# Two small edits at the ends of a tensor-bound kernel: a separate bank for the last half block, and narrower constant matmuls in the setup

## The chip, the cores and the metric

One NeuronCore of a Trainium2 chip. The metric is the device time of one execution in microseconds (us). The span in a profile is about 1.7 us shorter than the time of the same run (217.3 against 219.02 us before, 218.6 against 220.28 after). TensorE, VectorE, ScalarE and GpSimd are PE, DVE, ACT and POOL in the profile; SP is the engine that issues most transfers (111 of 120 in the profile of before).

## The reference, cut to what matters

A block-wise linear attention (4 batches, 8 heads, 768 tokens, head size 64) feeds a feed-forward layer with weights of 512 x 2048 and 2048 x 512.

```python
intra = einsum('bhic,bhjc->bhij', qb, kb) * Dmask     # scores inside a block
out   = einsum('bhij,bhjd->bhid', intra, vb) + (qb * lam_pow) @ kv_state
kv_state = lam_block * kv_state + kb_dec^T @ vb
x = out as (3072 tokens, 512)
h = x @ w_in;  g = h * cos(h);  y = g @ w_out
```

## The kernel before: the parts that matter

The kernel works on 24 blocks of 128 tokens. A planner in Python puts tasks of all engines in one order. The parts that the change and the argument touch:

```python
DMA_FROM = 8                      # from this block on q and k are transposed by DMA
...
def transposes_dma():             # block n >= DMA_FROM
    nc.sync.dma_start_transpose(out=new_T()..., in_=live["qk", n]...)
...
def scores():                     # waits for the transposed q and k of block n
    t = bank("ps_s", [P, 2, NP, P], F32)
    ... 8 matmuls of 128 columns ...
...
# last block: two column halves, both in the two-bank tile ps_s
live["f", i, j] = [bank("ps_s", [P, 2, DM], F32)[:, x, :width] for x in range(2)]
...
def keep_awake(us, at):           # constant matmuls while the setup has no work for the tensor engine
    for _ in range(int(us / (4 * P / (1200.0 if at < 5.0 else 2400.0) + 0.0025))):
        nc.tensor.matmul(idle_ps, lhsT=ident, rhs=blank, start=True, stop=True)
```

`keep_awake` is meant to keep the array's clock up until the first layer begins. It writes zeros that nobody reads.

## Time and profile before

| | before |
|---|---|
| time, four runs on the chip of the record, in order of size | 218.53, 218.69, 218.74, 222.54 us |
| span of the profiled run (a fifth run, of 219.02 us) | 217.3 us |
| tensor engine busy | 206.5 us, 95% |
| first matmul of the first layer | 21.21 us |
| wait for the DMA transpose of block 10 | 68.7 to 70.65 us |
| mean granted clock | 0.998 |

The tensor engine works almost without a break from 21 us to the end (two waits, 2.1 us in all, between 21 and 205 us). So the table's useful entries are the few times at which it does not: the stall near 18 us (1.11 us for which the profile shows no releaser, called the instruction stall below), the wait near 70 us and the gap between the two last groups. The lines are in the prediction.

### The profile page before, as it was taken

Reading aid. Unit: us, or ns where it says so; the run is one execution under the profiler, and the core shown is the slowest. Engines: PE = TensorE matmul, PEld = TensorE weight load, DVE = VectorE, ACT = ScalarE, POOL = GpSimd, SP = SyncE. Lnnn points to the kernel's source line nnn. Section 1 sums busy time; section 2 is a strip of 40 time slices with the busy share of each in tenths; the row PEclk is TensorE's granted clock in tenths of the full one; section 3 lists DMA queues with packets and bytes.
Section 4 is the critical chain, followed back from the end, with each engine's and each line's share of the span. In section 5 each row is a group of like instructions: output and inputs, shape, how many; then the busy total and the mean of one; then the engine's idle time right before and its main releaser. Section 6 shows DMA issues by size and latency. Waiting matters only on the chain.

```text
span 217.3 us, 4365 instructions
## 1 busy us (share of the span) xinstructions
PE 206.5 (95%) x1731; PEld 107.9 (50%) x1731; DVE 122.3 (56%) x217; ACT 106.7 (49%) x182; POOL 66.2 (30%) x85
## 2 busy tenths in 40 slices
PE   7797999999996999999999999999999999999993
PEld 2454444557664555454554445455454445555452
DVE  2694776456778677767765574674546334343200
ACT  5782775125664566464545435435444454445320
POOL 4594003786344545454444441300000000000000
PEclk9999999999999999999999999999999999999999
DMA  5999999999899999999899997201001101111112
GB/s 146 347 226 206 194 206 228 238 251 238 190 202 208 224 181 268 183 240 250 180 262 223 210 243 196 69 28 51 39 9 48 51 0 48 48 51 48 48 74 72
DMA packets 93588, 33.84 MB, mean 156 GB/s; under 512 B 80128, under 2 KB 90624, under 8 KB 93568
## 3 DMA queue, kind: packets, MB, share of 16 engines
q1 hardware_dynamic: 89200, 29.24, 58.8%
q0 software_dynamic: 4224, 4.19, 11.8%
q8 instruction: 13, 0.21, 0.4%
q10 hardware_dynamic: 144, 0.13, 0.2%
q14 instruction: 7, 0.06, 0.1%
HBM read 27.27 MB, written 6.29 MB: 154 GB/s over the span
## 4 chain that ended last, share of the span: by engine, by line
PE 89%; DMA 3%; DVE 3%; ACT 2%; issue 1%; POOL 1%; ACTq 0%
PE ps_f L620 36%; PE ps_h L577 26%; PE ps_t L577 10%; PE ps_s L331 3%; PE ps_o L356 3%; PE ps_o L360 2%; PE ps_f L577 2%; DMA qkT<-qk 2%; PE ps_s L620 2%; PE ps_o L620 2%; DVE s_m_sp L469 2%; DMA lam_bc<-in_lam_dram 1%; PE ps_h L680 1%; PE ps_kv L344 1%; POOL q_sp L432 1%
## 5 line engine op out<-in xcount | busy, mean ns | idle before, releaser
L620 PE MATMUL ps_f<-w_out_sb,g 128*128 128x512 bf16 x352 | 88.7, 379 | 0.3 <-ACT o_sb L632 0.2
L590 DVE TENSOR_TENSOR g<-ps_h,cos 128x512 bf16<-128x512 f32 (+2 forms) x77 | 47.2, 614 | 46.2 <-ACT cos L584 45.6
L584 ACT ACTIVATE cos<-ps_h,halfpi 128x512 f32<-128x512 f32 (+2 forms) x77 | 48.2, 626 | 49.4 <-PE ps_h L577 47.4
L577 PE MATMUL ps_h<-xT,w_in_sb 128*128 128x512 bf16 (+2 forms) x308 | 68.0, 349 | 0.0
L577 PEld LDWEIGHTS <-w_in_sb 128*128 128x128 bf16 x448 | 42.9, 98 | 41.4 <-issue 0.7
L620 PEld LDWEIGHTS <-g 128*128 128x128 bf16 x400 | 38.0, 98 | 39.6 <-issue 1.3
L274 POOL TENSOR_TENSOR qk<-q_f,q_scale 128x512 bf16<-128x512 f32 x20 | 20.8, 1042 | 51.8 <-DMA q_f<-in_q_dram 38.2
L584 ACT ACTIVATE cos<-ps_t,halfpi 128x512 f32<-128x512 f32 (+2 forms) x30 | 18.5, 616 | 20.6 <-PE ps_t L577 17.9
L338 DVE TENSOR_TENSOR s_m<-ps_s,mask 128x512 bf16<-128x512 f32 x40 | 26.2, 686 | 3.9 <-PE ps_s L331 3.5
L590 DVE TENSOR_TENSOR g<-ps_t,cos 128x512 bf16<-128x512 f32 (+2 forms) x30 | 18.0, 601 | 16.2 <-ACT cos L584 15.6
L577 PE MATMUL ps_t<-xT,w_in_sb 128*128 128x512 bf16 (+2 forms) x120 | 26.6, 344 | 0.0
L282 POOL TENSOR_TENSOR v_s<-v_f,v_scale 128x512 bf16<-128x512 f32 x20 | 20.8, 1042 | 11.5 <-DMA v_f<-in_v_dram 9.3
L632 ACT COPY o_sb<-ps_f 128x512 f32<-128x512 f32 x22 | 12.9, 585 | 20.1 <-PE ps_f L620 19.9
L350 DVE CAST kv_bd<-ps_kv 64x256 bf16<-64x256 f32 x32 | 13.4, 419 | 2.5 <-PE ps_kv L344 1.9
L278 POOL CAST qk<-k_f 128x512 bf16<-128x512 f32 x20 | 12.2, 609 | 2.8 <-DMA k_f<-in_k_dram 2.8
L366 ACT CAST xT<-ps_o 128x512 bf16<-128x512 f32 x20 | 11.6, 581 | 2.4 <-PE ps_o L360 2.3
L680 PE MATMUL ps_h<-blank,ident 128*128 128x512 bf16 x31 | 9.6, 441 | 1.6 <-POOL ident masks.py:199 1.6
L331 PE MATMUL ps_s<-qkT 64*128 64x128 bf16 x160 | 7.9, 219 | 1.9 <-DMA qkT<-qk 1.9
L360 PE MATMUL ps_o<-s_m,v_s 128*64 128x128 bf16 x160 | 7.9, 220 | 0.0
L356 PEld LDWEIGHTS <-kv_bd 128*64 128x64 bf16 x136 | 4.3, 109 | 6.7 <-issue 5.5
L356 PE MATMUL ps_o<-qkT,kv_bd 128*64 128x128 bf16 x136 | 7.0, 225 | 0.0
L331 PEld LDWEIGHTS <-qkT 64*128 64x128 bf16 x160 | 4.5, 94 | 3.4 <-DMA qkT<-qk 2.0
(88 smaller groups left out, 104.7 us busy)
## 6 DMA issues: line engine op xcount, KB each, us to landing
q_f<-in_q_dram SPq DMA_DIRECT2D x20, 256.0 KB, 3.9
k_f<-in_k_dram SPq DMA_DIRECT2D x20, 256.0 KB, 4.2
v_f<-in_v_dram SPq DMA_DIRECT2D x20, 256.0 KB, 4.4
out_dram<-o_sb SPq DMA_DIRECT2D x19, 256.0 KB, 2.0
w_in_sb<-in_moe_w_in_dram POOLq DMA_DIRECT2D x4, 512.0 KB, 8.0
w_out_sb<-in_moe_w_out_dram POOLq DMA_DIRECT2D x4, 512.0 KB, 14.1
out_dram<-o_sb SPq DMA_DIRECT2D x9, 128.0 KB, 2.7
q_f_sp<-in_q_dram SPq DMA_DIRECT2D x2, 512.0 KB, 5.1
```

Of the source, the lines that this page charges most:

```text
L274: (nc.vector if n == 0 else nc.gpsimd).tensor_mul(live["qk", n][:, 0], live.pop(("q_f", n)), q_scale[:, c, :].unsqueeze(2).to_broadcast([P ...
L282: nc.gpsimd.tensor_mul(live["v_s", n], live.pop(("v_f", n)), v_scale[:, c, :].unsqueeze(2).to_broadcast([P, H, D]))
L331: nc.tensor.matmul(t[:, i, p, :], lhsT=live["qkT", n][h, 1, p, :], rhs=live["qkT", n][h, 0, p, :], start=True, stop=True)
L338: nc.vector.tensor_mul(live["s_m", n][:, i], live["s", n][:, i], mask.unsqueeze(1).to_broadcast([P, NP, P]))
L350: (nc.scalar.copy if early else nc.vector.tensor_copy)(kv_bd[n % NK][h, :, h], kv_ps[h])
L356: nc.tensor.matmul(t[h, p, :], lhsT=kv_bd[(n - 1) % NK][:, p, h], rhs=live["qkT", n][:, 0, p, :], start=(p == 0), stop=False, skip_group_c ...
L360: nc.tensor.matmul(t[h, p, :], lhsT=live["v_s", n][:, 2 * p + i, :], rhs=live["s_m", n][:, i, p, :], start=(p == 0 and c == 0), stop=True, ...
L577: ins = nc.tensor.matmul(t[:, :cols], lhsT=w_in_sb[:, kd, f * P:(f + 1) * P], rhs=live["xT", i][:, kd, :cols], start=(kd == 0), stop=(kd = ...
L584: nc.scalar.activation(c[:, :cols], live["h", i, f][:, :cols], AF.Sin, bias=halfpi)
L590: nc.vector.tensor_mul(live["g", i][:, f, :cols], live.pop(("h", i, f))[:, :cols], live.pop(("c", i, f))[:, :cols])
L620: nc.tensor.matmul(live["f", i, j][piece], lhsT=live["g", i][:, f, j * P:(j + 1) * P], rhs=w_out_sb[:, f, part], start=(f == 0), stop=(f = ...
L632: (nc.scalar.copy if eng == "ACT" else nc.vector.tensor_copy)(o[:, :width], live["f", i, j][piece])
```

## The change

Its intent: let the second half of the last block start without waiting for the first half's copy, and use matmuls of 128 columns instead of 512 as constant work in the first 5 us, so that less of one can be in the way.

```diff
-    live["f", i, j] = ([bank("ps_s", [P, 2, DM], F32)[:, x, :width] for x in range(2)]
-                       if tag == "ps_s" else [bank(tag, [P, DM], F32)])
+    live["f", i, j] = [bank("ps_s", [P, 2, DM], F32)[:, 0] if tag == "ps_s" else bank(tag, [P, DM], F32)]
+elif f0 == 0:
+    live["f", i, j].append(bank("ps_t", [P, DM], F32))
 ... (each half now frees its own bank) ...
 def keep_awake(us, at):
-    for _ in range(int(us / (4 * P / (1200.0 if at < 5.0 else 2400.0) + 0.0025))):
-        nc.tensor.matmul(idle_ps, lhsT=ident, rhs=blank, start=True, stop=True)
+    cols = P if at < 5.0 else 4 * P
+    for _ in range(int(us / (cols / (1200.0 if at < 5.0 else 2400.0) + 0.0025))):
+        nc.tensor.matmul(idle_ps[:, :cols], lhsT=ident, rhs=blank[:, :cols], start=True, stop=True)
```

## The prediction

> **What bounds the kernel now.** I read four views, in this order. First the page, for the engines' shares and the chain of work that ended last:
>
> ```profile
> span 217.3 us, 4365 instructions
> PE 206.5 (95%) x1731; PEld 107.9 (50%) x1731; DVE 122.3 (56%) x217; ACT 106.7 (49%) x182; POOL 66.2 (30%) x85
> ...
> PE 89%; DMA 3%; DVE 3%; ACT 2%; issue 1%; POOL 1%; ACTq 0%
> ...
> L680 PE MATMUL ps_h<-blank,ident 128*128 128x512 bf16 x31 | 9.6, 441 | 1.6 <-POOL ident masks.py:199 1.6
> ```
>
> The tensor engine is the bound: it carries 89% of the chain, and every other engine is busy for about half the span or less. So only time in which it waits, or does work that isn't needed, can be won. The last row is the constant matmuls of the setup: 31 of them, of which the first 10 are those before 5 us that the change narrows.
>
> Second, what the tensor engine waited for over the whole run, longest first:
>
> ```profile
> PE ps_s L331 <- DMA qkT<-qk: 1.9, 1, 1.9
> PE ps_h L680 <- POOL ident masks.py:199: 1.6, 1, 1.6
> PE ps_s L494 <- issue: 1.1, 1, 1.1
> PE ps_t L443 <- DVE q_sp L432: 0.8, 1, 0.8
> PE ps_s L620 <- DVE o_sb L632: 0.5, 1, 0.5
> ```
>
> Few waits, each occurring once. The fifth is the one that the first half of the change goes for. The first and the third matter for the second half.
>
> Third, the tail, in order of time:
>
> ```profile
> 209.87 1.91 PE L620 MATMUL ps_s<-w_out_sb,g 128*128 128x256 bf16 x16
> ...
> 211.82 0.42 DVE L632 COPY o_sb<-ps_s 128x256 f32<-128x256 f32 x1 [7.48 <-PE ps_s L620]
> 212.30 1.91 PE L620 MATMUL ps_s<-w_out_sb,g 128*128 128x256 bf16 x16 [0.52 <-DVE o_sb L632]
> ...
> 214.29 0.37 ACT L632 COPY o_sb<-ps_s 128x256 f32<-128x256 f32 x1 [3.63 <-PE ps_s L620]
> 214.69 0.37 ACTq L640 DMA_DIRECT2D out_dram<-o_sb  x1
> ```
>
> The last block is computed in two column halves of 16 matmuls. The second half starts only when VectorE has copied the first half out, although the halves lie in two different banks: they are two slices of one two-bank tile, and the wait is on that tile. Everything after 209.87 lies on the chain, one thing after another, to the end.
>
> Fourth, the setup: the weight loads that go with the constant matmuls, and the tensor engine around 17 us.
>
> ```profile
> 4.15 0.15 PEld L680 LDWEIGHTS <-ident 128*128 128x128 bf16 x1 [0.28 <-issue]
> 4.58 0.15 PEld L680 LDWEIGHTS <-ident 128*128 128x128 bf16 x1 [0.28 <-issue]
> 4.94 0.10 PEld L680 LDWEIGHTS <-ident 128*128 128x128 bf16 x1 [0.21 <-issue]
> 6.29 0.17 PEld L443 LDWEIGHTS <-q_sp 128*128 128x128 bf16 x3 [1.26 <-DVE q_sp L432]
> ```
> ```profile
> 16.79 0.89 PE L494 MATMUL ps_s<-s_m_sp,v_sp 64*64 64x128 bf16 x31
> 18.80 0.21 PE L494 MATMUL ps_s<-s_m_sp,v_sp 64*64 64x128 bf16 x1 [1.11 <-issue]
> ```
>
> The constant matmuls start 0.43 us apart up to 4.58, and then faster: the array's clock comes up at about 4.8 us. They end near 5.4 us, and the first real work (a transpose of q) starts at 6.29, when VectorE has scaled q. In the second fence the last of 32 matmuls of a group starts 1.1 us after the others had ended, with no releaser[...].
>
> [...]0.43 us for 512 columns, and release about 3.2 us after the first matmul at 1.62.[...]
>
> **The change part by part.**
>
> *Second half in the bank of the transposes.* Removed: one wait. Same 16 matmuls, same copies, same stores; the bank was last read by the hidden layer's products long before. Sixteen matmuls take 1.91 us, of which the last one's own length is 0.27 (mean of the 128x256 row, 272 ns), so they start (1.91 - 0.27)/15 = 0.109 us apart. Without the wait the second half starts at 209.87 + 16 x 0.109 = 211.62 in place of 212.30: 0.68 us earlier. This is more than the 0.52 that the row shows as idle, because matmuls follow each other before the first has ended. Behind it come the ScalarE copy (0.37), the issue of the last store (0.37) and its landing; all shift with it. The first half's store is issued at about 212.3 and moves its data until about 213.5 by the DMA's share in fine stretches; the last store's data would begin near 214.7, so they don't collide. Gain: 0.68 us, wholly on the path.
>
> *Narrow constant matmuls.* Removed 10 of 512 columns, added 41 of 128 (the listing of instructions has 62 more on the tensor engine, 31 pairs). While the clock is held, 128 columns should take a quarter of 0.427, 0.107 us; 30 of them fill the 3.2 us to the release, the other 11 take about 0.056 each (the warm transposes of 128 columns start that far apart), together 3.2 + 0.6, so they end near 5.45 against 5.4. The next work waits for VectorE until 6.29 in both. Direct cost: zero.
>
> *The side effect of 62 more instructions.* [...]If the request escapes the weights' transfer, which begins just after 10.2, nothing stalls, and the next group starts when its other wait (a VectorE copy that ends at 17.7) allows: 1.1 us gained. So the first layer may start 0.5 to 1.1 us earlier.
>
> This should not reach the end. At 70.65 the tensor engine waits 1.9 us for a DMA transpose, and the queue that issues it runs without a pause:
>
> ```profile
> 61.72 1.17 SPq L638 DMA_DIRECT2D out_dram<-o_sb  x2
> 62.94 1.76 SPq L220 DMA_DIRECT2D q_f<-in_q_dram  x1
> 64.74 0.58 SPq L220 DMA_DIRECT2D k_f<-in_k_dram  x1
> 65.37 1.00 SPq L220 DMA_DIRECT2D v_f<-in_v_dram  x1
> 66.53 2.06 SPq L306 DMA_TRANSPOSE qkT<-qk  x1
> ```
>
> Each row begins where the one above ends, and so back to 32 us: the pace is the transfers', not the tensor engine's. What is won before 70 us makes that wait longer (2.4 to 3.0 us), and up to 1.9 us lost there would be hidden as well. I give the side effect 0.1 us.
>
> Sum: 0.68 + 0.0 + about 0.1 = 0.8 us, 0.36% of 218.74.
>
> **The rivals.**
>
> *The setup's gain passes through.* For it: stores of the first tile, in the same SP queue, wait for ScalarE's copies and so for the tensor engine; an earlier tensor engine might pull the queue forward. Against: the rows leave no gap to pull into. It would give up to 1.8 us in all, 216.9.
>
> *The narrow matmuls keep the clock down longer.* For it: they come with four times as many weight loads (0.15 us each while the clock is held, longer than the 0.107 of the matmul). If load and matmul did not overlap, 41 pairs would take over 6 us, run past 6.29 and push the transposes. Against: warm weight loads of 0.098 already hide behind transposes 0.056 us apart. Should it happen, up to about 1.9 us of it is absorbed at 70.65: 218.1 to 219.
>
> *A new wait in place of the old.* The copy of the second half waits for an output buffer and for the ScalarE queue too. Against: the copy would start at about 213.6, and the store that frees its buffer is the one three before, issued at 208.09 and landed by about 210 (2.0 us to landing on the page). Should the final store be held by the one before, the tail gains only 0.3 us: 218.4.
>
> *The fetch stall moves to a worse place in the dense part.*[...] Unlikely.
>
> **Range and chances.** 218.74 - 0.8 = 217.9 us. Below, the rival that passes through; above, a gain in the tail alone with noise: the three runs spread from 218.53 to 222.54, the last in a slower state that I don't predict. Eight in ten: 217.1 to 218.8. Two per cent is 4.4 us, six times what the tail holds: faster 1%, within 97%, slower 2%.
>
> **What would show it.** In the tail: no wait for VectorE in front of the second group, 32 matmuls without a break, and the last copy 0.68 us earlier relative to the group's start. In the setup: constant matmuls ending between 5.3 and 6.2 with the first transpose still at 6.29. Around 17 us: the wait without a releaser gone from the last matmul of that group, and either absent or at its first weight load. At 70 us: a longer wait for the DMA transpose, its landing unmoved. I am wrong if the second half still waits, if a start of the first layer that differs by more than 0.3 us arrives whole at the end, or if the clock comes up later than before.

## The result

On the chip of the record the changed kernel took 219.76, 220.28 and 220.51 us, and once 740.68 us; that run counts as of the slow state, is left out of the ratio, and no run explains it. The ratio to before is 1.007 (95% interval 1.0041 to 1.0099). A ratio here is the mean time of one kernel's fast runs over that of the other's in the same rounds, so it is not quite the ratio of the medians. The prediction was 217.9 with a range to 218.8: the change was to win 0.8 us and lost about 1.5.

The page of the changed kernel, cut to four lines:

```profile
span 218.6 us, 4399 instructions
PE 206.6 (95%) x1734; PEld 111.6 (51%) x1762; DVE 122.7 (56%) x217; ACT 106.8 (49%) x182; POOL 66.1 (30%) x85
...
PEclk9999999999999699999999999999999999999999
...
PE 84%; DMA 6%; DVE 5%; ACT 2%; issue 2%; POOL 1%; SPq 0%; ACTq 0%
```

The new thing is one digit in the clock row: a 6 in the fourteenth of 40 slices, 71 to 76.5 us. In the page of before that row was all nines. The chain's DMA share went from 3% to 6%.

The setup of the changed kernel, to be compared with the stall at 18.80 in the prediction; ahead of it, the first layer's start of before:

```profile
21.21 1.02 PE L577 MATMUL ps_h<-xT,w_in_sb 128*128 128x512 bf16 x4
```
```profile
16.80 0.90 PE L494 MATMUL ps_s<-s_m_sp,v_sp 64*64 64x128 bf16 x32
17.75 0.44 PE L476 MATMUL ps_kv<-v_sp,k_sp 64*64 64x64 bf16 x16
...
20.16 0.59 PE L577 MATMUL ps_h<-xT,w_in_sb 128*128 128x512 bf16 x2
```

All 32 matmuls of the group run on without a stall, the next group starts at 17.75, and the first layer at 20.16 instead of 21.21: 1.05 us earlier.

The tail of the changed kernel:

```profile
211.81 1.91 PE L620 MATMUL ps_s<-w_out_sb,g 128*128 128x256 bf16 x16
...
213.55 1.91 PE L620 MATMUL ps_t<-w_out_sb,g 128*128 128x256 bf16 x16
213.75 0.42 DVE L632 COPY o_sb<-ps_s 128x256 f32<-128x256 f32 x1 [7.48 <-PE ps_s L620]
215.54 0.37 ACT L632 COPY o_sb<-ps_t 128x256 f32<-128x256 f32 x1 [2.95 <-PE ps_t L620]
```

The second group starts 1.74 us after the first; before it was 2.43. That is the 0.69 us of the plan. But the first group starts at 211.81, before at 209.87. So between 20 and 210 us the changed kernel lost 1.05 + 1.94 = 2.99 us.

Where? First the chain of work around 70 us, before and after (start, length, what):

```profile
66.53 4.08 DMA qkT<-qk
...
70.65 0.40 PE ps_s L331 x8
```
```profile
66.92 4.05 DMA qkT<-qk
...
71.02 0.40 PE ps_s L331 x8
```

The DMA transpose is issued 0.39 us later and takes as long (4.05 against 4.08 us). So the 1.05 us are gone at 71 us, with 0.37 us more. Then the busy times in stretches (stretch; busy us and count of PE, PEld, DVE, ACT, POOL; granted clock; DMA share; GB/s). The first fence is the wait in the kernel before, the second the wait in the changed kernel and the 3.42 us after it:

```profile
68.70:70.60 1.90, 0.06 (x4) 0.00 (x0) 1.54 (x4) 0.92 (x2) 1.26 (x2) 1.00 0.98 182
```
```profile
68.30:71.00 2.70, 0.00 (x0) 0.00 (x0) 1.13 (x3) 0.37 (x1) 2.10 (x3) 1.00 1.22 240
71.37:74.79 3.42, 3.42 (x13) 1.61 (x12) 1.90 (x4) 1.16 (x2) 1.60 (x2) 0.50 1.29 194
```

The tensor engine idles for 1.89 us before and for 2.85 us after (68.17 to 71.02), and right behind the longer wait its clock is granted at 0.50 for 3.41 us. It is busy all that time, and the same work takes about twice as long (the eight matmuls of 384 columns behind the scores 2.67 us, before 1.41). So by my estimate it loses half of the 3.41 us, less what other waits would have taken. From 90 us on the two traces run in step at a distance of 1.94 us to the last block.

The account of the profiled pair: -1.05 at the start, +1.05 absorbed by the wait, +0.37 later landing, +1.57 half clock (1.94 - 0.37), -0.68 tail. The sum is +1.26; the spans differ by 218.57 - 217.31 = 1.26.

### The profile page after: what moved, and what is told of

It is laid out like the page before. It is cut to its first block, busy times and chain, and to the rows that moved or that the text cites. A ratio compares the mean times of both kernels' runs of the same rounds, so it can differ in the third digit from the quotient of the medians.

```text
span 218.6 us, 4399 instructions
## 1 busy us (share of the span) xinstructions
PE 206.6 (95%) x1734; PEld 111.6 (51%) x1762; DVE 122.7 (56%) x217; ACT 106.8 (49%) x182; POOL 66.1 (30%) x85
## 4 chain that ended last, share of the span: by engine, by line
PE 84%; DMA 6%; DVE 5%; ACT 2%; issue 2%; POOL 1%; SPq 0%; ACTq 0%
PE ps_f L620 33%; PE ps_h L577 26%; PE ps_t L577 9%; DMA qkT<-qk 4%; PE ps_s L331 3%; PE ps_o L356 2%; DVE s_m_sp L469 2%; PE ps_f L577 2%; PE ps_o L360 2%; PE ps_o L620 2%; DMA lam_bc<-in_lam_dram 1%; PE ps_t L620 1%; PE ps_s L620 1%; DVE v_sp L432 1%; PE ps_kv L344 1%
## 5 line engine op out<-in xcount | busy, mean ns | idle before, releaser
L620 PE MATMUL ps_f<-w_out_sb,g 128*128 128x512 bf16 x333 | 85.3, 379 | 1.7 <-issue 0.9
L577 PE MATMUL ps_h<-xT,w_in_sb 128*128 128x512 bf16 (+2 forms) x306 | 68.9, 354 | 0.2
L577 PEld LDWEIGHTS <-w_in_sb 128*128 128x128 bf16 x448 | 43.5, 99 | 42.5 <-issue 2.4
L278 POOL CAST qk<-k_f 128x512 bf16<-128x512 f32 x20 | 12.2, 609 | 0.7 <-DMA k_f<-in_k_dram 0.6
L680 PE MATMUL ps_h<-blank,ident 128*128 128x128 bf16 (+1 forms) x58 | 9.4, 333 | 1.8 <-POOL ident masks.py:199 1.6
L680 PEld LDWEIGHTS <-ident 128*128 128x128 bf16 x62 | 6.1, 132 | 2.7 <-POOL ident masks.py:199 1.6
```

The source lines that it names most:

```text
L577: ins = nc.tensor.matmul(t[:, :cols], lhsT=w_in_sb[:, kd, f * P:(f + 1) * P], rhs=live["xT", i][:, kd, :cols], start=(kd == 0), stop=(kd = ...
L620: nc.tensor.matmul(live["f", i, j][piece][:, :width], lhsT=live["g", i][:, f, j * P:(j + 1) * P], rhs=w_out_sb[:, f, part], start=(f == 0) ...
L680: nc.tensor.matmul(idle_ps[:, :cols], lhsT=ident, rhs=blank[:, :cols], start=True, stop=True)
```

## The experiments

My theory after the result: the setup half starts the first layer earlier, which only lengthens the wait for a transfer near 70 us, and a wait that long drops the clock. Rivals: the new bank in the tail costs something; the narrow matmuls themselves shift the clock; the chip was in another state.

### Each half alone

```diff
 # e1_tail: the changed kernel with the old keep_awake
 # e2_fill: the kernel before with the new keep_awake
```

> The first half of the change alone: second column half in its own bank, constant matmuls as before. My theory (the tail's gain is real; the loss comes from the setup half, which starts the first layer 1.05 us earlier, so that the wait for a DMA transpose near 70 us grows from 1.9 to 2.9 us and the array's clock falls to half for 3.4 us): 0.68 us faster than before, about 218.05; instruction stall of 1.1 us near 18 us still there; first layer's first matmul at 21.2; wait for the DMA transpose about 1.9 us, mean granted clock 0.998. Rival (the new bank in the tail costs time elsewhere, or the loss is a property of the chip's state in that hour): no faster than before, or clock 0.99 here too.

> The second half alone: narrow constant matmuls in the setup, tail as before. My theory: slower than before by about 2.0 us (the changed kernel's loss of 1.3 in the profile plus the tail's 0.68), about 220.7 to 221.1; no instruction stall near 18 us, first layer's first matmul at 20.2, wait for the DMA transpose near 71 us 2.5 to 3 us, clock 0.99, half clock for 3.4 us right after it. Rival (the two halves only hurt together): within 0.3 us of before.

Measured: the tail alone has a median of 218.91 us against 219.77 of before on this chip, ratio 0.9958 (0.9932 to 0.9985). The prediction's 0.68 us would be 0.9969. The constant matmuls alone: 221.10 us, ratio 1.0044 (1.0018 to 1.0071), a loss of 1.0 us, half of what was expected. So the halves are of opposite sign, and the loss belongs to the setup half. The tail's profile is at full clock with a longest wait for the transpose of 1.7 us; its instruction stall is 1.5 us, where 1.1 was expected.

Before is slower here than on the chip of the record (219.77 against 218.72) and spreads from 218.44 to 223.25 in 59 runs. I compare only inside a set.

The profile of the second kernel is the useful exception: it is of its fastest run (219.41 us), with a first layer at 20.35, and its clock stayed up after a wait of 2.4 us:

```profile
67.90:70.30 2.40, 0.00 (x0) 0.00 (x0) 1.47 (x4) 0.85 (x2) 1.96 (x3) 1.00 1.10 235
70.30:74.00 3.70, 3.66 (x28) 2.11 (x29) 2.55 (x5) 2.05 (x4) 1.72 (x3) 1.00 1.44 219
```

So a wait of 2.4 us need not drop the clock, although 13 of the 16 runs of the same program show a mean clock of 0.990 to 0.992, which is what one stretch of 3.41 us at half clock makes of it (half of 3.41 us is 0.8% of 217). What decides it comes below.

### Width or number of instructions

The change narrows the constant matmuls and also adds 62 tensor-engine instructions. This kernel leaves the first ten wide and cuts ten later ones in four, which adds 60.

```diff
+    parts = 4 if at >= 5.0 and split[0] > 0 else 1     # split[0] counts down from 10
+    cols = 4 * P // parts
+    for _ in range(parts):
+        nc.tensor.matmul(idle_ps[:, :cols], lhsT=ident, rhs=blank[:, :cols], start=True, stop=True)
```

> The tail of the change; the first ten constant matmuls 512 wide as before; the next ten (after 5 us) each cut into four of 128 columns, which adds 60 tensor-engine instructions ahead of the stall near 18 us, where the change adds 62. It tells the number of instructions from the width in the setup. My theory (only the number counts[...]): as the changed kernel: no stall at 18 us, first layer at 20.2, wait for the transpose 2.5 to 3 us, clock 0.99, 220.0 to 220.6. Rival (the narrow matmuls before 5 us, which ran wholly at half clock until 6.5 us in the changed kernel, are the cause): clock 0.998 and about 218.05 or less.

Measured: 219.98 us, ratio 0.9997 (0.9971 to 1.0023). Its profile is that of the changed kernel: no stall near 18 us, first layer at 20.36, a wait of 2.6 us, mean clock 0.99, 3.41 us at half clock from 70.8. One of twelve runs took 217.56, ten 219.6 to 220.6, and one, of the slow state, 222.80. So the number of instructions moves the stall, not the width. The traces show what goes with it. The instruction queue (q8) moved 13 packets of 16 KB in the kernel before, and the first of them starts at 16.4 us there and at 17.1 in the tail alone, but at 12.2 to 12.5 in the three kernels with 60 or 62 instructions more. That the stall is a wait for this packet is not shown: in the kernel before it had ended at 17.30, and the stalled matmul starts at 18.80. That it is requested earlier and so escapes the weights' transfer is not shown either; no run shows when it is requested.

### Busy in the wait

```diff
 def scores():
     t = bank("ps_s", [P, 2, NP, P], F32)
+    if n == 10:
+        for _ in range(12):
+            nc.tensor.matmul(t[:, 0] as 512 columns, lhsT=ident, rhs=blank, start=True, stop=True)
```

> The changed kernel with 12 constant matmuls of 512 columns (2.6 us) put in front of the scores that wait for the DMA transpose near 71 us, so that the tensor engine is busy during that wait. My theory (the idle time of 2.9 us is what drops the clock): clock 0.998, no half-clock stretch after 71 us, 1.6 us faster than the changed kernel, 218.6 to 219.0, with the data still arriving at about 71.0. Rival (the clock falls for another reason, such as the phase given by the narrow matmuls in the setup, or the time is lost in the wait itself): clock 0.99 and 220.4 as the changed kernel, or slower by the matmuls added.

Measured: 220.10 us, ratio 1.0001 (0.998 to 1.0023). The profile shows a mean clock of 0.999 and no half clock, as the theory has it, but the time came back by 0.3 us at most (the changed kernel has 1.0015, see below) instead of 1.6. For the clock a hit, for the time a miss. In the profile the transpose landed 4.8 us after its issue. Two more looks:

> A second look at the changed kernel with 12 constant matmuls in the wait near 71 us. If the late landing was chance: landing 3.7 to 4.1 us after the issue, the scores at 70.3 to 71.6. If a busy tensor engine always slows it: 4.6 us or more again, and no half clock.

> As the run before it, a third look; two of three late landings would make it the rule.

Both took 5.3 us, at full clock again; seven profiles of the other kernels show 3.7 to 4.1. So in three of three the clock was kept and the transfer was late by about 1.2 us. In a stretch around the transpose, the instruction queue (q8: packets, MB, share of 16 engines) moves one 16 KB block in this kernel, and none in the changed one:

```profile
q1 hardware_dynamic: 5344, 1.34, 114.4%
q8 instruction: 1, 0.02, 1.3%
```
```profile
q1 hardware_dynamic: 4165, 1.05, 123.6%
```

The packet's time is 1.3% of 16 DMA engines over 5.3 us, which is 1.1 us of one. That the constant matmuls bring it into the transpose and that it makes the transpose late is not shown; no run varies this packet alone. In the kept traces the two go together. Take the transpose of block 10 and the one after it (issued at 66.1 to 67.7 and at 70.6 to 72.4 us) in the ten profiles of kernels with this wait. In eight of these twenty a packet of the instruction queue was moving between issue and landing, and they took 4.64 to 5.78 us; the twelve without one took 3.70 to 4.31. Of all 32 DMA transposes in the profiles of before and after, the seven with a packet took 4.06 to 6.06 us, and the 25 without one 2.73 to 4.46.

### The changed kernel again, and its gain given back

```diff
 # e6_delay: the changed kernel, and before the first layer's first product
+    for _ in range(5):
+        nc.tensor.matmul(t, lhsT=ident, rhs=blank, start=True, stop=True)     # 1.08 us
```

> The changed kernel again, on the same chip as the three that follow. My theory now: the time is the landing of the tenth block's DMA transpose (70.3 to 72.1 us in the six traces so far) plus 142.5 us to the last matmul, plus 1.4 to 1.7 us in the runs in which the clock falls to half. So: ratio to before 1.00 to 1.007, most runs in a cluster 1.5 us above a few. Rival (the changed kernel is slower in all runs alike): one cluster.

> The changed kernel, its setup gain given back: five constant matmuls of 512 columns (1.08 us) right before the first layer, so that it starts at 21.2 to 21.4 as in the kernel before, without the stall near 18 us. My theory (the start 1.05 us earlier is what lengthens the wait and drops the clock): wait for the transpose near 71 us about 2 us again, most runs at full clock, ratio to before about 0.996, as the tail alone (0.9958), thus 0.5 to 1.5 us FASTER than the changed kernel although it only adds work. Rival (the narrow matmuls themselves[...] cost the time): as the changed kernel or 1 us slower.

Measured: the changed kernel 220.28 us, ratio 1.0015 (0.9988 to 1.0042); 22 runs from 217.67 to 221.64, its profile with 3.41 us at half clock and mean clock 0.99. The interval holds 1, so on this chip the loss of the record is not clear of noise. With 1.08 us of useless work added, 220.06 us, ratio 0.9982 (0.9954 to 1.0011), and a profile at full clock with a wait of 1.2 us near 70 us and one of 1.6 us for a later transpose. The sign is the theory's, the size (0.7 us) in the range expected, but the two intervals overlap, and over all 22 runs of each, slow ones included, the means differ by 0.35 us only: by their times alone these two are weak evidence.

The clock is better evidence than the time, for every run lists its mean, profiled or not. A mean of 0.984 to 0.992 stands for one or two stretches of 3.41 us at half clock in some 218 us. Counted over all runs, such a drop is in 16 of 22 of the changed kernel, 13 of 16 of the constant matmuls alone, 11 of 12 with later ones cut, 8 of 22 with the gain given back, and 0 of 20 with the tensor engine busy in the wait. Among the changed kernel's fast runs the 14 with a drop have a mean of 220.25 us, the six without 219.21.

One thing does not fit at first sight: the kernel before has a drop too, in 67 of 118 runs in the two sets on this chip, and the tail alone in 9 of 20. But there the fast runs with and without it differ by 0.3 us at most (219.98 against 219.66, 219.61 against 219.66, 219.28 against 219.01). A drop behind the instruction stall near 18 us, of which a profile below shows one, would lie ahead of the wait near 70 us and be hidden by it. No profile of these two kernels caught a drop, so this is not shown.

The eight profiles with this wait, up to here, in one table. The scores start when the transpose has landed. "Rest" is from there to the last matmul's start, with 0.68 us taken off where the tail has its old wait.

| kernel | scores start | last matmul | rest | half clock |
|---|---|---|---|---|
| before | 70.65 | 213.93 | 142.6 | no |
| tail alone | 71.60 | 214.10 | 142.5 | no |
| constant matmuls alone | 70.34 | 213.51 | 142.5 | no |
| busy in the wait | 72.06 | 214.57 | 142.5 | no |
| changed kernel | 71.01 | 215.19 | 144.2 | 3.41 us |
| changed kernel again | 71.26 | 215.24 | 144.0 | 3.41 us |
| later matmuls cut | 71.24 | 215.14 | 143.9 | 3.41 us |
| gain given back | 70.10 | 214.30 | 144.2 | no; a second wait of 1.64 us ends at 87.14 |

All are one law: landing of the transpose + 142.5 us, + 1.4 to 1.7 us where the clock fell, and in the last + 1.64 us for its second wait. The two further looks at the kernel that is busy in the wait have 142.5 too. Nothing of the setup's 1.05 us is in it.

### The wait taken away

If block 10 need not wait for a DMA transpose, the setup's gain has to show. In these two, blocks 8 to 10 are transposed on the tensor engine:

```diff
-DMA_FROM = 8
+DMA_FROM = 11
 # e5_from11: the changed kernel; e7_from11_wide: the same with the old keep_awake
```

> The changed kernel with the transposes of blocks 8, 9 and 10 on the tensor engine instead of by DMA: it takes the wait near 71 us away. Costs 24 transposes of 0.056 us (1.3 us) on the tensor engine. My theory: no wait over 1 us and no half clock near 71 us; the setup's gain of 1.05 us and the tail's 0.68 both reach the end: saves 2.9 + 1.6 us, costs 1.3: about 3 us faster than the changed kernel, ratio to before 0.987 to 0.992. Rival (the transfers bind all the way to 130 us, so that the wait only moves to the next block): a wait of 2 us for another transpose and a ratio of 0.996 to 1.005.

> The same with the constant matmuls of the kernel before (wide): blocks 8 to 10 transposed on the tensor engine, the tail's new bank, the instruction stall near 18 us back. With the wait gone, nothing should hide the setup's gain: my theory: 1.05 us slower than the run before it, a difference of 0.005 in the ratio. Rival (the setup's gain is absorbed elsewhere too): the two equal within 0.3 us.

Measured: 217.46 us, ratio 0.9906 (0.9871 to 0.994), all seven runs between 217.39 and 217.94. This version beats both kernels. Repeated on another chip:

> The version with blocks 8 to 10 transposed on the tensor engine again, as the base of the two that follow, which need its narrow spread. Both theories: 217.4 to 217.9, one cluster, clock 0.998.

217.62 us, ratio 0.9915 (0.9884 to 0.9946), six of seven within 217.39 to 217.72. The seventh, the profiled one, took 219.27: its clock came up only at 10.8 us (at 7.3 in the profile before), its first layer started only at 22.18 us instead of 20.33, and in this version that goes to the end (span 217.6 against 216.2). The expectation of one cluster was missed by this run.

With the old wide matmuls: 220.10 us, ratio 0.9996 (0.9972 to 1.002), in two groups of 22 runs: eight from 218.29 to 219.11 and fourteen from 219.94 to 220.59. The fast group's mean is 1.13 us above that of the narrow version (218.68 against 217.55), the 1.05 us that were expected. The slow group is 1.5 us above that, which was not. Its profile is of the slow group:

```profile
PE ps_s L494 <- issue: 1.5, 1, 1.5
```
```profile
20.55:23.96 3.41, 3.17 (x25) 0.50 1.24 206
```

(Stretch, PE busy and count, clock, DMA share, GB/s.) Right after the instruction stall of 1.5 us the clock is at half for 3.41 us. Ten of the fourteen runs of the slow group show a mean clock of 0.991 or 0.992; the other four (220.07 to 220.24 us) are at 0.999 or 1.000, so there something else cost the 1.5 us, and it stays open. So the setup half of the change is worth over 2 us on average where nothing behind it hides it.

### Idle made on purpose

The last version has a narrow spread, so an idle time can be added to it alone. In one kernel the scores of block 10 wait for five ScalarE copies; in the other the tensor engine is busy as long.

```diff
 if n == 10:
 # e8_idle
+    nc.tensor.matmul(t[:, 0] ..., lhsT=ident, rhs=blank, start=True, stop=True)
+    for _ in range(5): nc.scalar.copy(scratch, t[:, 0] ...)
 # e9_busy
+    for _ in range(15): nc.tensor.matmul(t[:, 0] ..., lhsT=ident, rhs=blank, start=True, stop=True)
```

> That base with an idle time made on purpose: before the scores of block 10 the tensor engine writes the bank once, ScalarE copies it out five times (5 x 0.585 us), and the scores wait for that: about 3.1 us of idle tensor engine. My theory (such an idle time drops the clock in most runs[...]): base plus 3.1 us in a minority of runs, base plus 4.5 to 4.8 us in most; profile, if of the majority, with 3.41 us at half clock and mean clock 0.99. Rival (idle time costs only itself): base plus 3.1 us in all runs, clock 0.998.

> The same place and the same time lost, but with the tensor engine busy: 15 constant matmuls of 512 columns (3.2 us). Both theories: base plus 3.2 us in all runs, one cluster, clock 0.998; my theory therefore 0.8 to 1.6 us FASTER in the mean than the idle one, the rival no difference.

Measured: busy, 220.84 us, all eight runs from 220.67 to 221.30, which is base plus 3.2. Idle, six runs: 220.91, 220.96, 222.36, 223.82, 223.86, 223.90. Same time lost, same place, and the idle one is 1.7 us slower in the mean. The steps are 1.45 us: none, one, two. I had expected one step only. The first profile was of the fast group, so two more looks:

> A second look at the idle time made on purpose. My theory: if the run is of the slow group (223.8), the clock is at half for one or two stretches of 3.41 us, the first of them beginning while the engine is idle near 77 us or right after; if of the fast group (220.9), the idle 3.1 us is split by a border of the 3.41 us grid into parts of less than about 2 us each. Rival: slow group at full clock, time lost elsewhere.

> As the run before it: a third look, for the group that is still missing.

They took 223.81 and 222.35 us. The same stretches in the three profiles, in the order of 220.91, 222.35 and 223.81 us:

```profile
77.65:80.20 2.55, 2.55 (x22) 1.00 1.12 282
80.20:83.60 3.40, 3.40 (x46) 1.00 0.55 119
```
```profile
77.65:80.20 2.55, 2.55 (x15) 0.50 0.43 74
80.20:83.60 3.40, 3.35 (x44) 0.94 0.00 0
```
```profile
77.65:80.20 2.55, 2.55 (x15) 0.50 1.15 290
80.20:83.60 3.40, 3.18 (x10) 0.50 0.20 43
```

Zero, one and two stretches of half clock behind the same 3.14 us of idle (74.5 to 77.65 us), and in all eight runs the mean clock goes with the group: 1.000, 0.992, 0.985. The clock records of the traces give the borders: in every trace that has them, all changes of the clock lie whole multiples of 3.413 us apart (in the changed kernel at 6.52, 71.37 and 74.79 us, 19 steps and one; in the slow run here at 5.12, 76.80 and 83.62, 21 and two), and the place of this grid relative to the program differs from run to run. In the fast run a grid border at 76.05 split the idle time into 1.6 and 1.6 us. In the middle run the border at 77.22 left 2.7 us in one grid window and 0.4 in the next. In the slow run the border at 76.80 left 2.3 and 0.85 us, and the second window, itself at half clock, was followed by another at half. The price comes out as half of what a half-clock window is busy: in the middle run 3.41 less 0.44 us of idle, halved, is 1.49 us, against 1.44 measured. The constant-matmuls-alone profile fits as well: its 2.4 us were split at 69.51 into 1.6 and 0.8. Of all windows at full clock after the first layer's start, none with 1.61 us of idle or less is followed by a drop, and each with 2.24 us (the kernel with later matmuls cut) or more is. So the line lies between these two, for the work that fills these windows. It is not a rule of idle time alone: the window of 17.13 to 20.55 us ahead of the drop in the wide version had 1.54 us of idle in all, the rest of it, by count, mostly small matmuls of 64 rows and 64 or 128 columns.

It follows that the kernel before was not plainly safe in its profile: a border at 69.72 split its wait of 1.89 us into two halves of 0.95. What 1.89 us in one window does, no profile shows.

## Why the prediction was wrong, point by point

- Tail: right. The second group started 0.69 us earlier relative to the first, without a break; the output without that wait is correct; the tail alone is 0.42% faster in the runs, where 0.31% was forecast.
- Direct cost of the narrow matmuls: right in the sum, wrong in a detail. All 41 ran at half clock and ended at 6.17 us, as the clock came up only at 6.52 in that run, against 4.86 before. The first transpose still started at 6.28. By the prediction's own list a later clock was a sign of being wrong, but the narrow matmuls do not do it: with them alone the clock came up at 4.66, with the old width and later ones cut at 5.97. So the 3.2 us from the first matmul to the clock are not fixed: in the changed kernel's profile they were 4.9 (1.62 to 6.52 us).
- The 62 instructions and the stall: right, at the upper end of 0.5 to 1.1 us, my estimate: 1.05 us, and the kernel with the old width and 60 more instructions shows that the number does it. The stall was not shortened but gone, and the first packet of the instruction queue came 3.9 us earlier (12.5 against 16.4).
- "This should not reach the end": right for the gain. The landing near 71 us does not follow the start of the first layer.
- The failing step: "What is won before 70 us makes that wait longer (2.4 to 3.0 us), and up to 1.9 us lost there would be hidden as well. I give the side effect 0.1 us." The wait did grow to 2.85 us (0.59 us because the tensor engine was there earlier, 0.37 because the data landed later). But a longer wait was priced as free, and it is not: all of it fell into one grid window and dropped the clock. The term that was to be -0.1 measured +1.94: 1.57 from the half clock and 0.37 from a later landing, a landing that scatters from profile to profile (scores from 70.1 to 72.2 us).
- The rival that had the clock in it looked at the setup only. The profile of before has the clock up behind the wait of 1.89 us and down from 216.49 us on, 2.28 us after the last matmul. A predicted gap of 2.4 to 3.0 us should have been held against these two, and some of the chance put on a loss; its size (1.5 us) only the later runs show.

A fetch stall in the dense part was called unlikely. In the profile of before the packets of the instruction queue lie 10.6 to 23.6 us apart there, and both waits between 21 and 205 us have a releaser.

What stays open: what the instruction stall waits for, whether an instruction fetch alone delays a transpose, the run of 740.68 us, the four runs of the wide version's slow group at full clock, where the old kernel's drops lie, and how its scatter on the other chips divides among its waits.

## What to carry to other kernels

Time won ahead of a wait for a transfer makes the wait longer, and on the tensor engine a longer wait can cost more than it hides (here a wait of 2.85 us in place of 1.89, and 3.41 us at half clock behind it, 1.57 us of the account): look at the length of every wait that a gain will feed. Remove the wait first and then harvest the gain ahead of it; here the two together, with the tail, gave 0.9%; the gain without the removal lost up to 0.7%, and the removal without the gain changed nothing (ratio 0.9996). Even instructions that run in idle time can move a stall behind them: with 60 or 62 more, the one of 1.1 to 1.5 us near 18 us was gone.
